# A partition split of one DMA load in a decode attention and MLP kernel: the fourth head of V in five pieces

## The chip, the core and the metric

The kernel runs on one core of one Trainium2 chip. Its time is the device time of one execution in microseconds (us). Three runs of the kernel before gave 102.31, 102.50 and 102.62 us; the median is 102.5 us. One further execution was recorded by the hardware profiler. The engines are named as the profile names them: PE is the matrix engine (PEld its weight loads), DVE the vector engine, ACT the scalar engine, POOL the general one, and SP the engine that issues most of the DMAs. SPq and ACTq are the instruction queues of SP and ACT as issuers of DMAs. The data itself is moved by 16 DMA engines that all the queues of the core share.

## What is computed

One token of a transformer layer in which attention and MLP stand side by side, all in bf16 with fp32 sums, batch 1, model width 1024:

```
xn  = layernorm(x)
q   = xn @ wq                                  # 32 heads of 128
k,v = the last 4096 of 65536 cached positions  # 4 kv heads of 128, 8 query heads share one
o   = softmax(q k^T / sqrt(128)) v
A   = o @ wo                                   # 4096 -> 1024
B   = gelu(layernorm(xn) @ w1 + b1) @ w2 + b2  # 1024 -> 3584 -> 1024
out = x + A + B
```

With one token every matrix is used once. K and V are 4 MB each for the window, wq and wo 8 MB each, w1 and w2 7 MB each; about 39.9 MB come from HBM in one execution.

## The kernel before

All large tensors pass through a ring of four SBUF buffers of 128 partitions by 16384 bf16 elements (the function `ring_tile`). In the order of the program the ring holds: K (all four heads), wq in two halves, a scratch buffer for transposing K, w1 in two halves, V (all four heads), w2 in two halves and wo in two halves. A load into a ring buffer is issued by SP (`nc.sync.dma_start`) as soon as the readers of the buffer's previous content are done.

Each of these loads spreads over the 128 partitions. For K and V, position p*32 + c of a head lies in partition p at column block c, so that each partition reads 32 positions of 128 elements, one contiguous run of 8 KB. A 128-partition load of one head is therefore 128 runs of 8 KB, 1 MB in all. V is loaded by three DMAs on line 212: heads 0 and 1 together, then head 2, then head 3. The second half of wo is cut along its rows into five DMAs (line 228) of 2 MB, 1 MB, 0.5 MB, 0.25 MB and 0.25 MB, so that the last one to land is small.

The compute side: the layernorms; K transposed in blocks by DVE (line 185) and its blocks moved by ACT and DVE (lines 199 and 201) into `kT`; q (line 237) and the first layer of the MLP (line 257) on PE; the scores (line 275), the softmax (lines 283 to 305), and the product with V (line 319), 32 matmuls that each read all four heads of one column block:

```
nc.tensor.matmul(o_all[:].rearrange("h g d -> h (g d)"), lhsT=eTb[:, 32 * c:32 * c + 32], rhs=v4[:, :, c, :],
                 start=(c == 0), stop=(c == NCH - 1))
```

Then w2 and wo are applied row block by row block. All but the last eight row blocks are summed into `accf` (line 338) and copied to `bulk` by DVE and ACT (lines 348 and 350). The last eight, those of the second half of wo behind its first 2 MB, are summed into `acct` (line 353). DVE adds the two (line 356), and SP stores the 2 KB result (line 357).

The order of instructions on each engine and all semaphores are set by a framework (Tile). Two things of it matter here. DMAs use eight completion semaphores in turn, numbered 100, 102, 103, 105, 106, 107, 109 and 110 in the trace; the issue of a DMA waits until the previous user of its semaphore has landed. And an instruction that needs several semaphores carries one wait itself, with further ones in separate wait instructions in front of it.

A completed load raises its semaphore once for each DMA engine that had a part in it, and the trace keeps the time of every such arrival, but not which engine sent it. The trace also holds the start, the length, the size and the queue of every DMA packet.

Of the kernel before, what the change touches and what calls it, by code (L numbers as in the profile page):

```python
# [16 lines left out]
def kernel(  # L17
# [14 lines left out]
    nc = tc.nc  # L32
    P = 128
    D = A_x.shape[-1]
    Hkv = A_k_cache.shape[1]
    Sk = A_k_cache.shape[2]
# [5 lines left out]
    W = min(4096, max(256, Sk // 4))  # L42
# [146 lines left out]
    for g in range(Hkv):  # L189
        T4 = scr[:, g, :].rearrange("p (c a j) -> p c a j", a=4, j=32)  # L190
        k = 0
        for R in range(4):
            for Cd in range(4):
                src = T4[32 * R:32 * R + 32, :, Cd, :]
# [12 lines left out]
        w1_tiles.append(tv)  # L207
    v_sb = ring_tile("v_sb")
    v4 = v_sb[:].rearrange("p (g c d) -> p g c d", g=Hkv, c=NCH)
    for g0, g1 in ((0, 2), (2, 3), (3, 4)):  # L210
        src = A_v_cache[0, g0:g1, Sk - W:Sk, :].rearrange("g (p c) d -> p g c d", p=P)
        nc.sync.dma_start(out=v4[:, g0:g1, :, :], in_=src)

    chunk_src = []
    w2_v = B_w2.rearrange("(p c) n -> p c n", p=P)
# [16 lines left out]
    for i, w3 in enumerate(wq_tiles):  # L232
        for r in range(4):
            c = 4 * i + r
# [16 lines left out]
    for i, w3 in enumerate(w1_tiles):  # L251
        for r in range(4):
            c = 4 * i + r
# [8 lines left out]
    for g in range(Hkv):  # L262
        b, th = divmod(g, 2)
        src = qT_ps[:, b * 4:(b + 1) * 4, 64 * th:64 * th + 64:32]
# [79 lines left out]
    for t in range(4):  # L344
        half, w = divmod(t, 2)
        src = accf[32 * half:32 * half + 1, 256 * w:256 * w + 256]
# [41 lines left out]
```

## Time and profile before

| what | value |
|---|---|
| median of three runs | 102.5 us |
| span of the profiled execution, first to last instruction | 100.7 us |
| median less span | 1.8 us |
| busy share PE, DVE, ACT | 49%, 49%, 34% |
| read from HBM | 39.86 MB, 396 GB/s over the span |
| first data packet of SP's queue, last packet of the last wo load | 1.82 us, 97.00 us |
| store of the result issued | 98.21 us |

The profile's page gives each engine's busy time, the span in 40 slices of about 2.5 us (a digit is the busy share in tenths), the DMA queues, the chain of work that ended last, the groups of instructions and the DMA issues. The chain is followed back from the last instruction: each piece is put down to what released it. The time of a DMA in the chain runs from its issue to its landing, so it includes the time in which it stands behind earlier loads in its queue. In the view of windows, the DMA share of a window is the sum of packet time over the window, divided by 16 engines; packets are counted in the window in which they start, so a share can be over 1 beside a neighbour that is under it.

### The profile page before, as it was taken

How to read it: one execution, taken by the hardware profiler on the slowest of the kernel's cores; microseconds unless marked ns; L12 is line 12 of the kernel's file. 1: busy time of each engine (PE TensorE's matmuls, PEld its weight loads, DVE VectorE, ACT ScalarE, POOL GpSimd, SP SyncE). 2: the span in 40 equal slices, each digit the busy share in tenths (PEclk: the TensorE clock that was granted, in tenths of full speed). 3: DMA queues.
4: the chain of work that ended last, by engine and by line, in shares of the span. 5: the costliest groups of instructions: out<-in, count | busy, mean ns of one | idle time of the engine just before them, and what ended most of it. 6: DMA issues, size and time to landing. Idle time of an engine off the chain costs nothing.

```text
span 100.7 us, 962 instructions
## 1 busy us (share of the span) xinstructions
PE 49.1 (49%) x361; PEld 19.2 (19%) x361; DVE 49.4 (49%) x91; ACT 34.2 (34%) x37; POOL 4.5 (4%) x18
## 2 busy tenths in 40 slices
PE   0027200008500930482882935999389930299830
PEld 0012200003100300121531222334133410023310
DVE  4335499999999999997126115510630000000130
ACT  0500002999999999962001045400000000000110
POOL 7105300000000000000000000000000000000000
PEclk9999999999985579555555555569976997559995
DMA  3899999999999998999999998999999998999910
GB/s 52 346 434 436 482 443 482 443 430 417 417 417 391 456 444 376 459 444 382 391 423 430 436 511 387 467 428 433 433 410 413 456 456 384 423 420 408 369 33 1
DMA packets 3031, 39.92 MB, mean 396 GB/s; under 512 B 458, under 2 KB 466, under 8 KB 851
## 3 DMA queue, kind: packets, MB, share of 16 engines
q1 hardware_dynamic: 2872, 39.85, 93.3%
q8 instruction: 3, 0.05, 0.2%
q10 hardware_dynamic: 154, 0.01, 0.1%
q14 instruction: 2, 0.01, 0.0%
HBM read 39.86 MB, written 0.00 MB: 396 GB/s over the span
## 4 chain that ended last, share of the span: by engine, by line
DVE 37%; DMA 24%; PE 19%; issue 9%; POOL 3%; ACT 2%; SPq 2%; POOLq 1%; DVEq 0%; ACTq 0%
DMA wo<-in_A_wo_dram 24%; DVE kt_scr L185 17%; DVE kT L201 16%; PE o_all L319 10%; PE sp L275 4%; PE acch L257 3%; SPq L228 2%; ACT e L297 1%; DVE eTb L299 1%; DVE m_loc L283 1%; PE qT_ps L261 1%; DVE q_sb L240 1%; POOLq L383 1%; ACT sc L280 1%; POOL spread L113 1%
## 5 line engine op out<-in xcount | busy, mean ns | idle before, releaser
L199 ACT COPY kT<-kt_scr 32x1024 bf16<-32x1024 bf16 x26 | 27.1, 1042 | 12.9 <-DVE kt_scr L185 12.6
L185 DVE STREAM_TRANSPOSE kt_scr<-k_sb 128x4096 bf16<-128x4096 bf16 x4 | 17.4, 4412 | 0.0
L201 DVE COPY kT<-kt_scr 32x1024 bf16<-32x1024 bf16 x38 | 15.9, 419 | 0.5
L237 PE MATMUL accq<-wq,xnT 128*1 128x512 bf16 x64 | 7.1, 622 | 17.9 <-DMA wq<-in_A_wq_dram 17.9
L350 ACT COPY bulk<-accf 1x256 f32<-1x256 f32 x2 | 0.7, 361 | 31.7 <-DVE bulk L348 31.7
L348 DVE COPY bulk<-accf 1x256 f32<-1x256 f32 x2 | 0.8, 416 | 21.3 <-PE accf L338 20.8
L319 PE MATMUL o_all<-v_sb,eTb 128*32 128x512 bf16 x32 | 9.9, 485 | 1.0 <-DVE zcol L310 1.0
L338 PE MATMUL accf<-wo,o 128*1 128x512 bf16 x48 | 7.1, 465 | 6.1 <-DMA wo<-in_A_wo_dram 6.1
L257 PE MATMUL acch<-w,yT 128*1 128x448 bf16 x64 | 6.3, 574 | 5.6 <-DMA w<-in_B_w_dram 5.6
L338 PE MATMUL accf<-w,hT 128*1 128x512 bf16 x56 | 7.9, 452 | 0.0
L237 PEld LDWEIGHTS <-xnT 128*1 128x1 bf16 x64 | 2.1, 115 | 22.1 <-issue 22.1
L319 PEld LDWEIGHTS <-eTb 128*32 128x32 bf16 x32 | 3.7, 119 | 6.8 <-issue 3.8
L338 PEld LDWEIGHTS <-o 128*1 128x1 bf16 x48 | 2.4, 98 | 10.8 <-issue 8.9
L275 PE MATMUL sp<-kT,qm 128*32 128x512 bf16 x32 | 3.8, 629 | 0.3 <-DVE qm L266 0.3
L257 PEld LDWEIGHTS <-yT 128*1 128x1 bf16 x64 | 2.0, 116 | 9.4 <-issue 9.4
L131 PE MATMUL ln_tot<-st,ones_f 128*128 128x1 f32 x2 | 0.6, 362 | 6.4 <-DVE st L129 6.4
L338 PEld LDWEIGHTS <-hT 128*1 128x1 bf16 x56 | 2.7, 96 | 4.7 <-issue 2.3
L322 DVE TENSOR_TENSOR o_m<-o_all,grs 32x512 f32<-32x512 f32 x1 | 0.7, 679 | 5.6 <-PE o_all L319 5.6
L297 ACT ACTIVATE e<-sc,nmx 128x1024 bf16<-128x1024 f32 x1 | 1.1, 1147 | 5.7 <-DVE nmx L294 5.7
L314 DVE STREAM_TRANSPOSE hT<-h_sb 128x896 bf16<-128x896 bf16 x1 | 1.7, 1711 | 2.4 <-ACT h_sb L312 2.4
L261 PE MATMUL qT_ps<-ident,q_sb 128*128 128x128 bf16 x8 | 1.2, 308 | 2.3 <-DVE q_sb L240 2.3
L275 PEld LDWEIGHTS <-qm 128*32 128x32 bf16 x32 | 2.1, 133 | 1.4 <-issue 0.9
(84 smaller groups left out, 34.4 us busy)
## 6 DMA issues: line engine op xcount, KB each, us to landing
w<-in_B_w_dram SPq DMA_DIRECT2D x4, 3584.0 KB, 26.1
wq<-in_A_wq_dram SPq DMA_DIRECT2D x2, 4096.0 KB, 21.6
k_sb<-in_A_k_cache_dram SPq DMA_DIRECT2D x4, 1024.0 KB, 7.1
wo<-in_A_wo_dram SPq DMA_DIRECT2D x1, 4096.0 KB, 29.4
v_sb<-in_A_v_cache_dram SPq DMA_DIRECT2D x1, 2048.0 KB
v_sb<-in_A_v_cache_dram SPq DMA_DIRECT2D x2, 1024.0 KB, 23.4
wo<-in_A_wo_dram SPq DMA_DIRECT2D x1, 2048.0 KB
wo<-in_A_wo_dram SPq DMA_DIRECT2D x1, 1024.0 KB, 23.1
```

The source lines that it names most:

```text
L185: nc.vector.transpose(out=scr[:, g, :], in_=k2[:, g, :])
L199: nc.scalar.copy(out=dst, in_=src)
L201: nc.vector.tensor_copy(out=dst, in_=src)
L228: nc.sync.dma_start(out=tv[:, a:b, :], in_=wo_v[:, nr * i + a:nr * i + b, :])
L237: nc.tensor.matmul(accq[32 * t:32 * t + 1, b, :], lhsT=xnT[:, c:c + 1], rhs=w3[:, r, j * 512:(j + 1) * 512], start=(c == 0), stop=(c == C ...
L257: nc.tensor.matmul(acch[32 * t:32 * t + 1, b, :NH], lhsT=yT[:, c:c + 1], rhs=w3[:, r, j * NH:(j + 1) * NH], start=False, stop=(c == C - 1) ...
L261: nc.tensor.transpose(qT_ps[:, b * 4 + hh, :], q_sb[:, b, hh * Dh:(hh + 1) * Dh], ident[:])
L275: nc.tensor.matmul(sp[32 * R:32 * R + 32, :], lhsT=qm[:, g, :], rhs=kT[:, g, c0:c0 + 512], start=(g == 0), stop=(g == Hkv - 1), tile_posit ...
L297: nc.scalar.activation(out=e128[:], in_=sc[:], func=ACT.Exp, bias=nmx[:], scale=scale, accum_out=l_loc[:])
L314: nc.vector.transpose(out=hT[:], in_=h_sb[:].rearrange("p (d c) -> p c d", c=CW2))
L319: nc.tensor.matmul(o_all[:].rearrange("h g d -> h (g d)"), lhsT=eTb[:, 32 * c:32 * c + 32], rhs=v4[:, :, c, :], start=(c == 0), stop=(c == ...
L338: nc.tensor.matmul(accf[32 * half:32 * half + 1, :], lhsT=vec[kind](c), rhs=wap[:, half * 512:(half + 1) * 512], start=False, stop=(idx == ...
```

## The change

One DMA for head 3 of V, 128 partitions, becomes five DMAs for the same bytes to the same places, for partitions 0 to 63, 64 to 93, 94 to 121, 122 alone, and 123 to 127. They are issued by SP in this order at the same place of the program. The other two loads of V, and all else, stay as they are.

```diff
-    for g0, g1 in ((0, 2), (2, 3), (3, 4)):
-        src = A_v_cache[0, g0:g1, Sk - W:Sk, :].rearrange("g (p c) d -> p g c d", p=P)
-        nc.sync.dma_start(out=v4[:, g0:g1, :, :], in_=src)
+    for g0, g1, p0, p1 in ((0, 2, 0, P), (2, 3, 0, P), (3, 4, 0, 64), (3, 4, 64, 94), (3, 4, 94, 122), (3, 4, 122, 123), (3, 4, 123, P)):
+        src = A_v_cache[0, g0:g1, Sk - W:Sk, :].rearrange("g (p c) d -> p g c d", p=P)[p0:p1]
+        nc.sync.dma_start(out=v4[p0:p1, g0:g1, :, :], in_=src)
```

## The prediction

> **What bounds the kernel now.** I read the slices first, then the queues, the chain, the waits of SP's queue, and last the windows at the tail. The times of single packets and semaphore arrivals quoted further down are from the trace's packet and arrival records.
>
> ```profile
> DMA  3899999999999998999999998999999998999910
> q1 hardware_dynamic: 2872, 39.85, 93.3%
> DVE 37%; DMA 24%; PE 19%; issue 9%; POOL 3%; ACT 2%; SPq 2%; POOLq 1%; DVEq 0%; ACTq 0%
> 73.20 24.12 DMA wo<-in_A_wo_dram
> 97.32 0.04 issue
> 97.36 0.31 PE acct L353 x4
> ```
>
> The first line says that the 16 DMA engines are busy from about 2 to 97 us without a hole, the second that nearly all of it is SP's queue (q1). The chain names DVE most, but that part is K's transposition, beside which loads go on. What sets the end is the piece of 24.12 us: the last wo load, issued at 73.20, stands behind all earlier loads and lands at 97.32. Behind it only four small matmuls, one addition and the store follow, 3.4 us to the end of the span. So the kernel ends when the slowest of the 16 DMA engines is through its queue, and the windows show how uneven that is:
>
> ```profile
> 95.00:95.20 0.20, 0.20 (x12) 0.18 (x8) 0.11 (x1) 0.00 (x0) 0.00 (x0) 1.00 1.08 420
> ...
> 96.20:96.40 0.20, 0.20 (x8) 0.08 (x1) 0.00 (x0) 0.20 (x1) 0.00 (x0) 1.00 0.13 51
> 96.40:96.60 0.20, 0.09 (x4) 0.00 (x0) 0.00 (x0) 0.01 (x1) 0.00 (x0) 1.00 0.13 51
> 96.80:97.00 0.20, 0.20 (x4) 0.02 (x4) 0.00 (x0) 0.00 (x0) 0.00 (x0) 1.00 0.06 20
> ```
>
> The last but one column is the DMA share. From 96.2 us it is 0.13, two engines of 16; at the end 0.06, one. The arrivals of the last load agree: 13 engines between 95.53 and 96.10, one at 96.28, and two late ones, call them A at 97.11 and B at 97.32. They differ by little else than two accidents that the packet records show. The page's queue q8 holds three instruction fetches of 16 KB; the first, at 45.89, took 936 ns on A, and A's next 28 KB packet took 1556 ns in place of 1062; the second, at 67.55, did the same to B (938 and 1551). Each costs its engine 0.94 + 0.49 = 1.4 us for good, as no engine takes over rows of another. The third starts at 95.89 on an engine that has nothing left to do.
>
> **What the change moves.** Head 3 is 128 packets of 8 KB at 309 ns, eight on each engine. Every load in the trace is shared out equally: 128 partitions raise the semaphore 16 times, four (the store) four times, two (xb) twice and one (b1) once. By equal shares I estimate 64 partitions at 4 on 16 engines, 30 at 2 on 15, 28 at 2 on 14, 1 on one, 5 on five. The engine that took b1's 272 ns row also took xb packets, so small loads begin on the same engine rather than in turn. Then one engine gets 10 packets for 8 (+0.62 us), four get 9 (+0.31), nine stay at 8, one gets 6 (-0.62) and one 4 (-1.24).
>
> [...]
>
> Which engines are these? Engines that took b1 and xb belong to the eight whose first K load arrived first (packet ends at 4.98 to 5.23); A and B belong to the other eight (5.29 to 5.43). If the two groups are the lower and upper half, the late two are among those that get no more, and I take it that they are the two lightened ones (chance 0.55). The nearest row, the group of eight, does not prove it; the bounds are -1.24 and +0.62 for each.
>
> With A at -0.62 and B at -1.24: 96.49 and 96.08. With them swapped: 95.87 and 96.70. The engine of b1, among the 13 (its packets end at 95.68, arrival near 95.97), rises to 96.61, and the one at 96.28 at most to 96.59. So the queue would end at 96.6 to 96.7 for 97.32, 0.6 to 0.7 us sooner.
>
> **What is late next.** The third fetch starts 1.0 us after the matmuls of line 353 begin at 94.88. That start waits for the 0.5 MB piece of wo, which would be some 0.6 us sooner; the fetch comes then at about 95.3, when its engine, idle before by 95.89, is mostly still at work (arrivals 95.53 to 96.10). Its price is 1.41 us as on A and B, at least 0.61 (what a 16 KB packet of wo takes). An unchanged engine with arrival 95.75 would end between 96.36 and 97.16. I take the upper part, since both rows of a fetch within work show the full price, and for the engine at about 97.05: a gain of 0.27 us in place of 0.65. If it falls on an engine already done, the 0.65 stay; on the engine with +0.62 the end is 96.61 + 1.41 = 98.0, a loss of 0.7.
>
> **Edits priced at nothing.** Four more issues, at 388 to 478 ns on this line, take 1.8 us of SP, from 37.67 to 39.5; SP's next issue, on line 220, is at 44.97, and without those 5 us it would be late by the 1.8. The semaphores in turn shift by four:
>
> ```profile
> SPq L90 <- DMA x_sb<-in_A_x_dram: 3.1, 1, 3.1
> ```
>
> The first wq load needs nothing of x, but its semaphore was x's; it waited for that. After the change the fifth piece of V takes the first w1 half's (landed 41.73), and SP stands until then with w2 behind it. The first w2 half takes the second w1 half's, landed at 50.93: issued at 51.0 for 44.97. A queue with V in it until 58.7 covers that by 7 us; from a bare queue, K's first packet came 1.0 us after its issue. The second w2 half waits for V's heads 0 and 1 (55.8 for 46.5, cover until 67), the first wo for head 2 (58.2 for 58.14, cover until 75). With no cover these delays would be paid whole: 6, 9 and 0.1 us.
>
> The product with V waits for seven V loads, not three, two wait instructions more at 51 ns. V's last arrival is 60.64, now perhaps 0.5 us sooner or later; PE waits for DVE until 61.47 anyway, and what depends on it, the wo issues at 71.40, has until 85.3. A further completion packet is 9 ns, overlapping 3: 4 x 6 = 24 ns on the engine with all five.
>
> [...] Here the two last wo pieces, 0.25 MB each, are 0.64 us apart, the time of their eight packets of 84 ns: no fixed part on a full queue.
>
> **The sum** against the profiled execution: 100.7 - 0.27 + 0.02 = 100.45 of span; the median stands 1.8 us above it: 102.25 us.
>
> **The rivals.**
>
> (1) The third fetch stays harmless: a gain of 0.6 to 0.65, 101.85 us. For it: a third or so of the engines are near their end by 95.3. Against: 13 engines are above 95.5 by arrival. Chance 0.22.
>
> (2) The late two are not both the lightened. With only B lightened A's 97.11 stands, a gain of 0.21; with only A, or neither, nothing: 102.3 to 102.5. For it: eight engines in their group; against: nothing in the profile. Chance 0.28. [...]
>
> (3) Slower: the third fetch falls on one of the five engines that were given more. It decides as soon as such an engine has packets left when the fetch comes; with +0.31 it ends at 95.84 to 96.59 plus 1.41, that is 97.25 to 98.0, with +0.62 at 98.0: -0.1 to +0.7, so 102.4 to 103.2 us, taken at 103.0. For it: five of the 14 other engines. Against: the fetch lies late, and a price below 1.41 takes it away. Chance 0.17.
>
> (4) The five pieces do not spread as I estimate, or a semaphore wait lets the queue run dry after all: 102.6 to 103.5. Chance 0.08.
>
> My forecast, the fetch on an unchanged engine, has 0.25, with 102.0 to 102.6 of its own.
>
> **How the numbers follow.** A change of under 0.3% (0.31 us) cannot be told from none here; the three runs before span that much. Faster by more: (1) whole, a half of the forecast's 0.25 with the fetch early or cheap, 0.35. Same: the other half, nearly all of (2), a third of (3) with +0.31 alone, 0.42. Slower: the rest of (3), (4) and a few hundredths of (2) where a late engine is among the five given more (+0.31), 0.23. The range reaches from 101.75 (rival 1 with 0.1 us of scatter) to 103.0 (most of rival 3), leaving out the worst of (3) and (4) and some of (1).
>
> **What the profile after would show.** Semaphore arrivals of the five pieces numbering 16, 15, 14, 1 and 5 prove the split. SP's issue of w2 at about 51 us and full DMA slices throughout prove the waits covered. If the windows at the tail go from full to nothing within half a microsecond, the two late engines were lightened; two engines alone for the last microsecond mean they were not. A 16 KB packet of q8 before 95.7, and one engine alone 1.4 us behind the rest, is the forecast's own mark. The prediction is wrong if the fetches move to other engines between executions, or if the late ones are elsewhere.

## The result: 107.1 us for 102.5

The changed kernel takes 107.1 us (median of four runs, 106.99 to 107.27) where the kernel before takes 102.5 us. The ratio is 1.0458, with a 95% interval of 1.0436 to 1.0479. The forecast was 102.25 us with a range of 101.75 to 103.0, so the result lies 4.1 us above the end of the range. The span of the profiled execution grew from 100.7 to 105.4 us.

The views that were read before, now of the changed kernel. From its page, the slices, the queue of SP and the chain by engine:

```profile
DMA  2999999999999899998999998999999999999810
GB/s 53 373 434 426 510 398 398 485 497 410 398 398 511 359 416 446 392 474 354 416 438 317 241 188 322 457 413 441 413 457 455 410 410 416 429 398 419 332 39 1
q1 hardware_dynamic: 2907, 39.85, 93.1%
DMA 80%; PE 12%; SPq 4%; issue 1%; DVE 0%; DVEq 0%
```

And pieces of the chain in order of time (start, length, what):

```profile
38.26 27.30 DMA v_sb<-in_A_v_cache_dram
65.56 0.04 issue
65.60 9.14 PE o_all L319 x32
...
76.55 25.25 DMA wo<-in_A_wo_dram
```

The kernel before had in the same slices:

```profile
GB/s 52 346 434 436 482 443 482 443 430 417 417 417 391 456 444 376 459 444 382 391 423 430 436 511 387 467 428 433 433 410 413 456 456 384 423 420 408 369 33 1
```

The DMA engines are as busy as before: the slices show no hole, and q1 takes the same share. But for about 10 us, in four slices from the 22nd on, they move 317, 241, 188 and 322 GB/s where about 420 is usual. Busy engines that move half are engines whose packets take longer. The chain shows the place: a piece of V, issued at 38.26, lands only at 65.56, and the product with V starts then. Windows of 1 us around it (the last column is GB/s, the one before it the DMA share) for the kernel before, and then for the changed one:

```profile
57.00:58.00 1.00, 1.00 (x12) 0.14 (x4) 0.00 (x0) 0.00 (x0) 0.00 (x0) 0.50 1.01 426
60.00:61.00 1.00, 0.26 (x2) 0.18 (x2) 0.83 (x1) 0.14 (x2) 0.00 (x0) 0.50 1.00 430
```

```profile
54.00:56.00 2.00, 1.30 (x25) 0.65 (x29) 1.26 (x6) 0.00 (x0) 0.00 (x0) 1.00 1.02 430
...
58.00:59.00 1.00, 0.22 (x2) 0.14 (x2) 0.54 (x1) 0.43 (x2) 0.00 (x0) 1.00 1.00 213
59.00:60.00 1.00, 0.00 (x0) 0.00 (x0) 1.00 (x4) 0.13 (x1) 0.00 (x0) 0.78 1.13 242
60.00:61.00 1.00, 0.00 (x0) 0.00 (x0) 0.00 (x0) 1.00 (x1) 0.00 (x0) 0.50 1.12 213
...
66.00:67.00 1.00, 1.00 (x4) 0.42 (x3) 0.00 (x0) 0.00 (x0) 0.00 (x0) 0.50 1.00 430
```

Before head 3 of V the rate is 430 GB/s, with head 3 it is 213 to 242, and 430 again once the w2 packets right behind it are through.

The packet records give the size of the loss. Before, every one of the 512 packets of 8 KB of V took 309 ns. Now 121 of them take more than 330 ns, with a median of 624, just above twice 309. Summed over the engines they take 41.0 us more than 309 each. The w2 packets of 28 KB that come behind them take up to 2756 ns for 1062, and 28.3 us more in all. By engine that is 41.0 / 16 = 2.56 us and 28.3 / 16 = 1.77 us, 4.33 together. The last load of the kernel lands 4.48 us later (101.80 for 97.32). What follows it takes 0.2 us longer, which comes from a detail at the end of SP's program:

```profile
SPq L383 <- DMA out_dram<-res: 0.7, 1, 0.7
```

```profile
SPq L383 <- DMA out_dram<-res: 1.1, 1, 1.1
```

These are from the waits of SP's queue, first of the kernel before, then of the changed one. At the end SP waits for all DMA semaphores in a fixed order, 105 first and 110 last. Before, the store of the result had semaphore 110 and was waited for last; with four DMAs more it has 105, and four further wait instructions, some 60 ns apart, run after it has landed. From the landing of the store to the end of the span it is 0.84 us before and 1.08 us after.

### The profile page after: what moved, and what is told of

Same layout as the page of the kernel before. It is cut to its first block, busy times and chain, and to the rows that moved or that the text cites. A ratio compares the mean times of both kernels' runs of the same rounds, so it can differ in the third digit from the quotient of the medians.

```text
span 105.4 us, 969 instructions
## 1 busy us (share of the span) xinstructions
PE 47.1 (45%) x361; PEld 18.7 (18%) x361; DVE 49.3 (47%) x91; ACT 34.2 (32%) x37; POOL 4.5 (4%) x18
## 4 chain that ended last, share of the span: by engine, by line
DMA 80%; PE 12%; SPq 4%; issue 1%; DVE 0%; DVEq 0%
DMA v_sb<-in_A_v_cache_dram 26%; DMA wq<-in_A_wq_dram 25%; DMA wo<-in_A_wo_dram 24%; PE o_all L319 9%; DMA x_sb<-in_A_x_dram 5%; PE accq L237 3%; SPq L212 2%; SPq L228 2%; DVE res L356 0%; SPq L90 0%; PE acct L353 0%; DVEq L356 0%
## 5 line engine op out<-in xcount | busy, mean ns | idle before, releaser
L199 ACT COPY kT<-kt_scr 32x1024 bf16<-32x1024 bf16 x26 | 27.1, 1042 | 13.0 <-DVE kt_scr L185 12.7
L319 PE MATMUL o_all<-v_sb,eTb 128*32 128x512 bf16 x32 | 9.1, 455 | 6.9 <-DMA v_sb<-in_A_v_cache_dram 6.9
L338 PE MATMUL accf<-wo,o 128*1 128x512 bf16 x48 | 7.8, 501 | 4.8 <-DMA wo<-in_A_wo_dram 4.8
L257 PE MATMUL acch<-w,yT 128*1 128x448 bf16 x64 | 4.8, 463 | 5.8 <-DMA w<-in_B_w_dram 5.8
```

The lines of the kernel that those rows point to most:

```text
L199: nc.scalar.copy(out=dst, in_=src)
L257: nc.tensor.matmul(acch[32 * t:32 * t + 1, b, :NH], lhsT=yT[:, c:c + 1], rhs=w3[:, r, j * NH:(j + 1) * NH], start=False, stop=(c == C - 1) ...
L338: nc.tensor.matmul(accf[32 * half:32 * half + 1, :], lhsT=vec[kind](c), rhs=wap[:, half * 512:(half + 1) * 512], start=False, stop=(idx == ...
```

## Experiments

Three theories stood at the start. P: the pieces address only a part of the partitions, and the 16 engines that write into it get a part of the rate. W: the number of DMAs and the waits of their semaphores. U: the unequal shares of the engines. In each run only the loop of line 212 differs from the kernel before. Of each edit the lines that matter are shown. Where head 3 has a loop of its own, the loop of line 212 keeps the other two loads, and `v3` is head 3 as 128 rows, one for each partition. "Extra packet time" below is worked out from the packet records as above: the 8 KB packets of V over 309 ns each plus the w2 packets over 1062 ns each, divided by 16 engines.

**Five column pieces.** All 128 partitions in each piece, as many DMAs and the same waits as after the change.

```diff
-    for g0, g1 in ((0, 2), (2, 3), (3, 4)):
+    for g0, g1, c0, c1 in ((0, 2, 0, NCH), (2, 3, 0, NCH), (3, 4, 0, 16), (3, 4, 16, 23), (3, 4, 23, 30), (3, 4, 30, 31), (3, 4, 31, 32)):
...
+        nc.sync.dma_start(out=v4[:, g0:g1, c0:c1, :], in_=src)
```

> Head 3 of V in five DMAs of 128 partitions each, cut along the columns (16, 7, 7, 1 and 1 of the 32 column blocks) instead of along the partitions. The number of DMAs, their order, the semaphores in turn and so all waits of SP are those of the changed kernel; each DMA has all 16 engines and the usual assignment of partitions to them. Theory P (few partition groups: 16 engines that write into half of the partitions at a time get half the rate, as the 213 to 242 GB/s between 58 and 61 us after the change against 430 elsewhere suggest): 102.5 us, within 0.3. Theory W (number of DMAs and the later issue of w2, 51.08 for 44.97 us): near 107. Theory U (unequal shares of the engines, 15, 14, 1 and 5): 102.5.

Measured: 103.3 us, ratio 1.0086 (1.0056 to 1.0116). The w2 packets are back at 1062 ns, apart from the one that an instruction fetch hits. So neither the number of DMAs nor the late issue of w2 makes the 4.6 us; 0.9 of them could be of that kind, which a later run takes up.

**Two halves.** One DMA more than before, equal shares.

```diff
+    for g0, g1, p0, p1 in ((0, 2, 0, P), (2, 3, 0, P), (3, 4, 0, 64), (3, 4, 64, 128)):
```

> Head 3 in two DMAs of 64 partitions, 0 to 63 and 64 to 127: equal shares of four 8 KB packets on each of 16 engines in both, and only one DMA more than before. Theory P: each half MB at about 213 GB/s, the whole MB 4.9 us for 2.45, so at least 2.5 us more, 105.0 to 107. Theory W: one DMA more and little change of waits, 102.5 to 103. Theory U: shares are equal, 102.5.

Measured: 106.39 us, ratio 1.0364 (1.031 to 1.0417). The windows:

```profile
57.00:58.00 1.00, 0.65 (x6) 0.50 (x2) 0.16 (x1) 0.06 (x1) 0.00 (x0) 0.73 1.02 197
58.00:59.00 1.00, 0.00 (x0) 0.00 (x0) 0.00 (x0) 1.00 (x2) 0.00 (x0) 1.00 0.94 188
59.00:60.00 1.00, 0.22 (x2) 0.14 (x2) 0.79 (x1) 0.18 (x2) 0.00 (x0) 1.00 1.07 221
```

Half the rate at a full DMA share, with only two equal pieces: 126 packets of 8 KB have a median of 624 ns. The extra packet time is (41.0 + 20.3) / 16 = 3.83 us of the 4.0 lost. W and U fall as the main cause; a plain cut in two halves costs nearly all that the five pieces cost.

**Four quarters.**

```diff
+    for g0, g1, p0, p1 in ((0, 2, 0, P), (2, 3, 0, P), (3, 4, 0, 32), (3, 4, 32, 64), (3, 4, 64, 96), (3, 4, 96, 128)):
```

> Head 3 in four DMAs of 32 partitions. Theory P in the form in which the rate goes with the number of partitions addressed at once: a quarter of the rate, 9.8 us for 2.45, 109 to 112. [...] Theory W: 103 to 106, three DMAs more. Theory U: equal shares, 102.5.

Measured: 106.29 us, ratio 1.0375 (1.0343 to 1.0407), the same as two halves. The long packets have a median of 605 ns. So between 64 and 32 partitions the rate does not go with their number: 32 of them are as good, or as bad, as 64 (605 ns a packet for 624).

**Eight pieces of 16 partitions.**

```diff
+    for g0, g1, p0, p1 in ((0, 2, 0, P), (2, 3, 0, P), (3, 4, 0, 16), (3, 4, 16, 32), ..., (3, 4, 112, 128)):
```

> Head 3 in eight DMAs of 16 partitions, one 8 KB packet on each engine in each. [...] Theory U: 102.5.

Measured: 107.89 us, ratio 1.0535 (1.0486 to 1.0583). Its windows:

```profile
57.00:58.00 1.00, 0.04 (x1) 0.00 (x0) 0.16 (x1) 0.66 (x1) 0.00 (x0) 1.00 0.99 148
58.00:59.00 1.00, 0.22 (x2) 0.14 (x2) 0.39 (x1) 0.58 (x2) 0.00 (x0) 1.00 1.10 172
...
60.00:61.00 1.00, 0.00 (x0) 0.00 (x0) 0.15 (x1) 0.98 (x1) 0.00 (x0) 0.50 0.99 156
61.00:62.00 1.00, 0.00 (x0) 0.00 (x0) 0.00 (x0) 0.99 (x3) 0.00 (x0) 0.50 0.40 66
62.00:63.00 1.00, 0.00 (x0) 0.00 (x0) 0.49 (x1) 0.47 (x1) 0.00 (x0) 0.50 0.49 148
```

Two things are in it. The long packets have a median of 792 ns, longer than the 624 of the halves, and the rate is 148 to 172 GB/s. Why 16 contiguous partitions cost more than 32, and 32 no more than 64, is not shown. And the DMA share falls to 0.40: here the queue did run dry. Eight pieces take all eight semaphores in turn, w2 had to wait for the first piece of head 3 itself and was issued at 62.28. The engines stand idle for 19.5 us in all between 60 and 65 us, 1.2 per engine; with (51.2 + 12.7) / 16 = 4.0 us of extra packet time that is 5.2 of the 5.5 us.

**Which side, source or destination?** A half of the partitions is also a contiguous half of the MB in HBM. Two runs separate the sides. In the first each half of the partitions is filled from every other row:

```diff
...
+    v3 = A_v_cache[0, 3, Sk - W:Sk, :].rearrange("(p c) d -> p c d", p=P)
+    for i in range(2):
+        nc.sync.dma_start(out=v4[64 * i:64 * i + 64, 3, :, :], in_=v3[i:P:2])
```

> Two DMAs of 64 partitions as in the run with halves, but the first reads the even rows of head 3 and the second the odd ones, so each reads 8 KB runs spread over the whole MB while it writes one half of the partitions (the rows of V come to other partitions than the reference has them, so the result is another; the bytes and the work are the same). Theory D (the destination: 16 engines write into half of the partitions at a time): as the halves, 106 to 106.5, 8 KB packets of about 624 ns. Theory S (the source: 16 engines read one contiguous half MB at a time): 102.4 to 103, packets of 309 ns.

Measured: 105.95 us, ratio 1.0358 (1.0291 to 1.0425), 205 GB/s between 57 and 59 us, long packets with a median of 609 ns. In the second each contiguous half MB goes to all partitions:

```diff
...
+    for i in range(2):
+        src = A_v_cache[0, 3, Sk - W + 2048 * i:Sk - W + 2048 * (i + 1), :].rearrange("(p c) d -> p c d", p=P)
+        nc.sync.dma_start(out=v4[:, 3, 16 * i:16 * i + 16, :], in_=src)
```

> Two DMAs of 128 partitions, each into half of the columns of head 3, each reading one contiguous half MB in runs of 4 KB (the positions come to other partitions than the reference has them, so the result is another; the bytes and the work are the same). The number of DMAs and the bytes of each are those of the run with halves. Theory D: 102.4, within 0.4, packets of 159 ns as the 4 KB pieces of wo. Theory S: 105.5 to 106.5, packets of about 320 ns. If one more DMA by itself costs something, it shows here too.

Measured: 102.35 us against 102.4, ratio 0.9991 (0.9969 to 1.0013). All its 256 packets of 4 KB take 159 ns. Windows of the one that writes halves, then of the one that reads halves:

```profile
57.00:58.00 1.00, 1.00 (x13) 0.20 (x5) 0.00 (x0) 0.00 (x0) 0.00 (x0) 0.50 1.10 205
58.00:59.00 1.00, 0.53 (x6) 0.44 (x2) 0.16 (x1) 0.18 (x1) 0.00 (x0) 0.50 0.89 205
```

```profile
57.00:58.00 1.00, 1.00 (x16) 0.23 (x8) 0.00 (x0) 0.00 (x0) 0.00 (x0) 0.50 1.01 414
59.00:60.00 1.00, 0.00 (x0) 0.00 (x0) 0.00 (x0) 0.90 (x1) 0.00 (x0) 0.50 1.07 455
```

The destination makes the loss; one more DMA costs nothing here.

**Two heads in halves.**

```diff
+    for g0, g1, p0, p1 in ((0, 2, 0, P), (2, 3, 0, 64), (2, 3, 64, P), (3, 4, 0, 64), (3, 4, 64, P)):
```

> Heads 2 and 3 both in two halves of 64 partitions. In the run with one head in halves the 8 KB packets took 41.0 us more in all, 2.56 per engine, and the w2 packets behind them 20.3, 1.27 per engine. If theory D holds with the w2 part paid once, at the border to the next load: 102.4 + 2 x 2.56 + 1.27 = 108.8, between 108.3 and 109.3. If every border between halves and other loads costs its own: 102.4 + 2 x 3.9 = 110.2. If the loss were a fixed price of a load cut in parts late in the queue: 106.4.

Measured: 108.62 us, ratio 1.0604 (1.0567 to 1.064); 108.8 was expected from a price per packet plus one border. The extra packet time is (72.5 + 19.2) / 16 = 5.73 us. The w2 part is as large as with one head in halves (20.3), the V part nearly twice (72.5 for 41.0). So halves cost by the byte, and the border to the next load once. At the border, engines which are through with head 3 begin on w2 while others still write halves: in the changed kernel the first w2 packet starts at 59.31, and head 3 has landed at 65.56. That this overlap is what slows the w2 packets is argued, not shown.

**Even and odd partitions.** 64 partitions in each DMA, but every second one.

```diff
...
+    for i in range(2):
+        nc.sync.dma_start(out=v4[i:P:2, 3, :, :], in_=v3[i:P:2])
```

> Head 3 in two DMAs of 64 partitions, the even ones and the odd ones, result as the reference. If what counts is that a DMA has only 64 partitions: 106.4. If what counts is whether its partitions reach all groups of four neighbours, which the even ones do: 102.5. [...]

Measured: 102.53 us, ratio 1.0009 (0.9985 to 1.0033). All 512 packets of 8 KB of V take 309 ns. Its windows:

```profile
57.00:58.00 1.00, 0.61 (x6) 0.50 (x2) 0.16 (x1) 0.09 (x1) 0.00 (x0) 0.50 1.03 434
59.00:60.00 1.00, 0.27 (x2) 0.18 (x2) 0.82 (x1) 0.15 (x2) 0.00 (x0) 0.50 1.19 512
```

So 64 partitions are no fault in themselves. Spread over the whole array, they moved at the full rate, 434 to 512 GB/s in these windows. That it is groups of four neighbours that count is not shown: the run says that every second partition is spread enough.

**The shares of the change, spread.** If strided pieces are free, the uneven shares can be had without the halves.

```diff
...
+    for p0, n, st in ((0, 64, 2), (1, 30, 4), (3, 28, 4), (115, 4, 4), (121, 2, 4)):
+        p1 = p0 + (n - 1) * st + 1
+        nc.sync.dma_start(out=v4[p0:p1:st, 3, :, :], in_=v3[p0:p1:st])
```

> Head 3 in five DMAs of 64, 30, 28, 4 and 2 partitions, each strided (every second or every fourth partition) so that each but the last two reaches groups of four neighbours all over the array; the result is the reference's. The shares of the engines are nearly those of the changed kernel (10, 10, 9, 9, eight on ten engines, 6 and 4), and so are the number of DMAs and the waits of SP. If the whole loss came from the halves: no loss is left, at most 0.4 us, and the 8 KB packets stay at 309 ns. Then the rest of the prediction is tested by itself: if the two late engines are those with 6 and 4 packets, the tail shrinks by 0.3 to 0.65 us, 101.8 to 102.1; if they are others, as the early arrival of the lightened engines in the changed kernel's trace says, 102.4, within 0.3. If part of the 4.6 us came from unequal shares, five DMAs or the waits, it is left here: 103 or more.

Measured: 104.41 us, ratio 1.0192 (1.0154 to 1.023). The loss is halved, not gone: the 64 even partitions run nearly clean, then 52 packets of 8 KB take 330 to 704 ns, and the w2 packets behind them up to 2122. The extra packet time is (11.8 + 19.0) / 16 = 1.92 us, the whole loss. The packet times are measured; why strided pieces with unequal shares have long packets is not shown, for which engine wrote where is not in the trace.

**Two more distributions of that kind,** ten and six packets on the two halves of the engines, and ten, eight and four:

```diff
+    for p0, n, st in ((0, 64, 2), (1, 32, 4), (3, 8, 4), (35, 8, 4), (67, 8, 4), (99, 8, 4)):
...
```

> Head 3 in six strided DMAs of 64, 32, 8, 8, 8 and 8 partitions: ten 8 KB packets on the first eight engines, six on the last eight; the result is the reference's. If the two late engines of the kernel before are both among the last eight (the prediction's argument from the two groups of first arrivals), both are relieved by 0.62 us and the tail ends at about 96.7 for 97.32: 101.8. If one of them is among the first eight: 102.9 to 103.0. If the fetch at the end now falls on an engine still at work, up to 0.5 us of the gain is gone. The fifth and sixth piece wait for the landing of the two w1 halves, and w2 is issued at about 56 us with V in the queue until 58.7; if that runs dry, 103 and more.

```diff
+    for p0, n, st in ((0, 64, 2), (1, 24, 4), (3, 24, 4), (97, 8, 4), (99, 8, 4)):
...
```

> Head 3 in five strided DMAs of 64, 24, 24, 8 and 8 partitions: ten packets on the first eight engines, eight on the next four, four on the last four; the result is the reference's. If both late engines are among the last four, they are relieved by 1.24 us, and the first eight set the end at up to 96.1 + 0.62: 101.8 to 101.9. If they are among the four that keep eight: 102.4. If one is among the first eight: 103.0.

Measured: 103.46 us, ratio 1.0101 (1.0069 to 1.0132), and 104.57 us, ratio 1.0213 (1.0175 to 1.0252). The extra packet times are (1.1 + 11.9) / 16 = 0.81 us and (11.5 + 17.6) / 16 = 1.82 us. Both expectations missed: the longer packets, 0.81 and 1.82 us per engine, cost more than the 0.6 us or so that a better balance was expected to give, so these two times do not say where the two late engines are. The packet records of the first run do, for that execution. The engine that the first fetch delays (at 46.05) has six packets of head 3: its parts of the first two pieces end at 59.23 and 60.31 us, and its next packet is one of w2. The engine that the second fetch hits (at 67.29) has ten, as far as packets can be told apart. So the two are not both among the last eight. That the fetches hit the same engines in every execution is not shown.

**Seven whole loads.** What of the 0.9 us of the five column pieces is due to the number of DMAs?

```diff
+    for g0, g1, c0, c1 in ((0, 1, 0, 32), (1, 2, 0, 32), (2, 3, 0, 32), (3, 4, 0, 8), (3, 4, 8, 16), (3, 4, 16, 24), (3, 4, 24, 32)):
```

> V in seven DMAs of 128 partitions: heads 0, 1 and 2 whole, head 3 in four pieces of eight column blocks (runs of 2 KB, no small ones). SP issues as many DMAs as in the changed kernel, its seventh piece waits for the first w1 half and the first w2 load for the second w1 half, as there; only the second w2 half has less to wait for. The run with five column pieces was 0.9 us slower than the kernel before. If that came from the waits and the number of DMAs: again 103.0 to 103.4. If it came from its runs of 256 and 1792 bytes: 102.4 to 102.7, of which 0.1 is for the 2 KB runs (84 ns a packet against a quarter of 309).

Measured: 103.24 us, ratio 1.0102 (1.0078 to 1.0126), so it is not the runs of 256 bytes alone. In the profiled execution the span is 0.72 us longer than before. Of that, 0.24 is the end of SP's program told above (the store has semaphore 105 here too), and 0.49 is the later landing of the last load. Head 3's 512 packets of 2 KB took 46.7 us for 128 x 309 ns = 39.6, 0.45 per engine: 0.22 because 84 ns is more than a quarter of 309, and 0.23 because some took up to 380. The five column pieces lost 0.47 in the same way. Apart from the start and the tail, the queue shows no hole of more than 0.04 us per engine, though w2 was issued at 51.09. So the waits are hidden, as the prediction had it; each of the other parts is a consequence of cutting the load or of the rotated semaphores. The median's 0.92 us is 0.2 more, because the kernel before had a median of 102.32 us beside this run, and the profiled execution that the spans are compared with took 102.5.

The price of a layout can be read off the packets of the runs that keep rows of 8 KB:

| run | extra packet time, us per engine | median less the median before, us |
|---|---|---|
| changed kernel | 4.33 | 4.6 |
| two halves | 3.83 | 4.04 |
| four quarters | 3.22 | 3.94 |
| eight of 16 | 3.99, and 1.2 of idle queue | 5.54 |
| halves, rows mixed | 3.06 | 3.55 |
| two heads in halves | 5.73 | 6.22 |
| the change's shares, spread | 1.92 | 1.97 |
| ten and six | 0.81 | 1.02 |
| ten, eight and four | 1.82 | 2.13 |
| even and odd | 0.03 | 0.13 |

The first column is a mean, while the kernel ends with the slowest engine; that, and up to 0.24 us at the end of SP's program, fits a second column that is always the larger one. No version was faster than the kernel before; those that read half of the source at a time, or write even and odd partitions, are as fast (ratios 0.9991 and 1.0009).

## Why the prediction was wrong

**What bounds the kernel** was right: the DMA queues, and their slowest engine. Of the 4.7 us by which the span grew, 4.5 are in that queue.

**The step that failed** is the price of the moved packets. The prediction took 309 ns for every 8 KB packet of head 3 whatever engine moved it, and so made the change a matter of counts, -1.24 to +0.62 us on single engines. 121 packets of V took more, 624 ns in the middle, and those of the next load up to 2.6 times their usual time. That is a term of +4.3 us per engine, in the mean, which the sum did not have. In the trace of before every load addresses 128 partitions, save the small ones of x and b1 and the store, so no row showed a large load on fewer. The bounds given, -1.24 and +0.62, took the packet time for fixed, and it was the packet time that needed a bound. The prediction's argument that the queue shows no fixed part per DMA holds (one more DMA cost nothing in the run that reads half the source at a time, 102.35 us for 102.4), but it bears on the number of DMAs and not on what the runs show: the halves measured 188 to 221 GB/s for some 430. What in the chip makes a contiguous half of the partitions that slow, no run shows.

**The shares** were right. The five pieces raised their semaphores 16, 15, 14, 1 and 5 times.

**The late engines** were placed wrongly, as far as the traces with unequal shares tell. Followed packet by packet through the changed kernel's trace, the engine with 4 packets of head 3 (the one that starts on w2 first, at 59.31) and, as far as packets can be told apart, the one with 6 were not hit by a fetch; they came first at the end, the last load's arrivals being 99.11 and 99.68, then ten between 99.86 and 100.21, and four late ones up to 101.80. So the lightened engines were not among the late ones there. Windows at the tail (DMA share and GB/s at the end):

```profile
99.50:100.00 0.50, 0.50 (x18) 0.30 (x12) 0.05 (x1) 0.00 (x0) 0.00 (x0) 1.00 0.48 184
100.00:100.50 0.50, 0.34 (x10) 0.13 (x3) 0.36 (x1) 0.05 (x1) 0.00 (x0) 1.00 0.25 98
101.00:101.50 0.50, 0.29 (x8) 0.09 (x4) 0.26 (x1) 0.20 (x1) 0.00 (x0) 1.00 0.11 41
```

A share of 0.25 is four engines where the forecast's balance would have left none. Among the cases about balance it is the rival that the late two are others, at 0.28, that fits, and so does the run with ten and six packets, where the two engines that the fetches hit had six and ten. The prediction's argument from two groups of first arrivals, which put both late engines in the same half, does not hold there. That this half is the one that gets no more was the author's estimate; the traces do not number the engines.

**The third fetch** did not decide. It began at 100.91, and the four late engines were late by as much in the 1 MB piece before (98.45 to 99.34, the others by 97.72). The prediction let the matmuls of line 353 wait for the 0.5 MB piece; in the trace of before they start at 94.88, 0.04 us after the last arrival of the 1 MB piece (94.84), and the 0.5 MB piece lands at 96.06. The two late engines are last in both, so its sum does not hang on this.

**The waits** were right in time and cover. SP's issues in order of time:

```profile
36.02 5.99 SPq L212 DMA_DIRECT2D v_sb<-in_A_v_cache_dram  x7
51.08 5.22 SPq L220 DMA_DIRECT2D w<-in_B_w_dram  x2
60.55 16.45 SPq L228 DMA_DIRECT2D wo<-in_A_wo_dram  x6
```

The fifth piece was issued at 41.76 and w2 at 51.08, as worked out (41.73 and 51.0), and the queue stayed full. The eight pieces of 16 show what happens without cover: w2 at 62.28, and 1.2 us of idle engines. What the prediction missed at the same place is the end of the program, 0.24 us for a store that has another semaphore.

**The product with V** was priced at nothing, with V landed at about 60.6 and DVE awaited until 61.47 anyway. V landed at 65.56. This delay has no part in the loss, since the wo issues it holds back (74.76) still stand in a queue whose w2 packets run until 82.0.

**The rival for a slow-down by the pieces' spread** (chance 0.08, up to 103.5) had no mechanism and too small a price. Its sign was right.

## What to carry to other kernels

On a full DMA queue like this one, a large load into SBUF should address partitions all over the array, in equal shares on all 16 engines. A contiguous half or quarter of the partitions moved at half the rate here (8 KB packets of 624 and 605 ns for 309) and slowed the load behind it too, while a cut along the columns into runs of 4 KB (159 ns a packet), or into even and odd partitions (309 ns for 8 KB), moved at the full rate. Runs of 2 KB cost 0.45 us per engine, and strided pieces with unequal shares lost 1.0 to 2.1 us in all. Before a load is cut, look for the packet time of a load of that shape, not only for packet counts; where the trace has none, bound the packet time itself. With a framework that uses its semaphores in turn, count which earlier load each later issue then waits for, to the very last wait of the program.

## What the runs showed of the hardware beyond that

- An instruction fetch of 16 KB cost its DMA engine 1.4 us on the full queue of the kernel before: 936 ns for itself and 494 more on the next 28 KB packet (1556 for 1062), and 938 and 489 the second time. The fetches made two of 16 engines end 0.8 and 1.0 us behind the third-latest (97.11 and 97.32 for 96.28).
- 32 contiguous partitions and 64 cost the same (packets of 605 and 624 ns), 16 cost more (792 ns), and 64 strided by two cost nothing (309 ns, as in loads of 128).
- Uneven shares on strided partitions slowed the load behind them even where their own packets were hardly slowed: with ten and six packets the V packets took only 1.1 us more in all, the w2 packets 11.9.
